# Cosformer attention and a mixture of adapters: K cast once, V weighted instead of K and Q, Q cast by GpSimd transfers, in a new schedule

## The chip, the cores and the metric

The kernel runs on one core of one Trainium2 chip. The metric is the time of one execution on the device, in microseconds (us); lower is better. The engines are named as in the profile: PE multiplies matrices (PEld is its weight load), DVE is the vector engine, ACT the scalar engine, POOL is GpSimd, and SP issues transfers. The transfers themselves are carried out by 16 DMA engines.

## The reference

The inputs q, k and v have the shape (8, 8, 576, 64): batches, heads, positions, features, in 32-bit floats. The attention is linear, and positions are weighted by a cosine and a sine. Its result is reshaped to 4608 rows of 512 features and goes through a mixture of eight low-rank adapters, of which each row takes its best two:

```python
theta = np.pi / 2.0 * pos / S
def phi(x, c, s):
    r = np.maximum(x, 0.0)
    return np.concatenate([r * c, r * s], axis=-1)
q_p, k_p = phi(q, cos_w, sin_w), phi(k, cos_w, sin_w)
kv  = np.einsum('bhsf,bhsd->bhfd', k_p, v)
num = np.einsum('bhsf,bhfd->bhsd', q_p, kv)
den = np.einsum('bhsf,bhf->bhs', q_p, k_p.sum(2))[..., None] + 1e-06
x = num / den                      # then to (4608, 512)
logits = x @ w_gate                # two largest of eight, softmax over the two: w
out = x + sum over the two e of w * ((x @ A[e]) @ B[e])
```

The sum over k_p is had by a column of ones beside v, so that kv has 65 columns.

## The kernel before

Position s is split as s = 9 p + j: p runs over 64 partitions (two heads fill 128), and j = 0 to 8 over the free dimension. A load (line 435, on SP's queue) brings q, k or v of one or two batches in this layout; one batch of one tensor is 1152 KB. The work goes by units of batches: [0], [1], [2,3], [4,5], [6,7] (line 20). For each unit the loads are K, V, Q in this order.

For each j of K and of Q a step `phi` multiplies by the cosine and by the sine of the position and writes bf16, two instructions of 256 columns (one batch) or 512 (two). For K it applies the relu as well, for Q not. It runs on ACT (line 487), DVE (490) or POOL (493). V is cast once, two instructions of 1152 columns a batch (`vc`, lines 360 to 362 by the engine), into `vb` with its column of ones. `kv` (line 540) is 72 matmuls a batch: 64 partitions of one head and one j contract 128 weighted features of K with 65 columns of V; both row halves of the array are used. `ke` copies kv out of PSUM.

The output is made in 36 tiles of 128 rows. A tile holds two blocks of 64 positions, from two batches or from two values of j. Per tile there are: `tq`, eight 128x128 transposes of weighted Q (line 650); `eq`, the relu on the way from PSUM to `qt`, 1024 columns a tile, mostly two tiles at a time (line 668, on DVE); `nd`, 16 matmuls of 65 columns in column halves of the array (line 691) and four narrow ones that add the epsilon (698); `rd` and `nx`, the reciprocal and the product into `x` (717, 722, DVE); `tx`, four transposes (742); `ex`, the copy into `xt` (358 on ACT, 362 on DVE); `za`, four matmuls with adapters A and gate (767). Then, for a group of up to three tiles, come the small steps of the choice of two: `mx` on DVE (778), `nt` on POOL (790), `ge` and `d` on DVE (799, 794), `sg`, a sigmoid, on ACT (804), `w` on POOL (807), `zg` on DVE (810). `tz` and `ez` transpose and copy the result; `dx` adds x and the adapters' output with two matmuls of 512 columns a tile (850, 852); `eo` copies the sum into `o` (358), and SP stores it (868). Matmuls at line 878 are fillers that keep PE busy in gaps.

The order is made by a planner (`plan`, line 124) that runs once, while the program is built: each step has engines with costs, buffers that it takes and frees, and a key; the planner simulates the engines and places what can start first. The result is one fixed order for each engine, and each engine works in that order, also when a step has to wait. A load is planned only when no more than 11.34 us of transfers are queued (`BACKLOG`, line 88). Staging for K and Q has two tiles of two batches each.

Of the kernel before, what the change touches and what calls it, by code (L numbers as in the profile page):

```python
# [14 lines left out]
AXL = mybir.AxisListType  # L15

NJ = 9
UNITS = [[0], [1], [2, 3], [4, 5], [6, 7]]  # L20
# [11 lines left out]
class Res:  # L32
    def __init__(self, name, n):
        self.name = name
        self.free = [0.0] * n
        self.held = [False] * n

    def reset(self):
        self.log = []
        self.free = [0.0] * len(self.free)  # L40
        self.held = [False] * len(self.held)

    def best(self, cnt, align, allowed=None):
        pick = None
        for s in range(0, len(self.free) - cnt + 1, align):
            if allowed is not None and s not in allowed:
                continue
# [24 lines left out]
class Op:  # L72
    def __init__(self, name, key, engs, deps, emit, alloc=(), free=(), dma=0):
        self.name, self.pos, self.engs, self.deps = name, key, engs, list(deps)
        self.emit, self.alloc, self.free, self.dma = emit, alloc, free, dma
        self.eng = None
        self.chain = None
        self.mode = 0
        self.sb = False
        self.pen = {}  # L80
        self.t0 = self.t1 = None
# [7 lines left out]
FILL_FROM = 4.0  # L89


EQ_TAIL, ND_TAIL, EX_TAIL, EO_TAIL = 2, 2, 2, 1
LAST_GROUPS = (3, 3, 2, 1)

A_TQ = {1: (4, 5, 6, 7), 2: (4, 6)}
A_ND = {1: (0, 2), 2: (0,)}
A_KV = (2, 4)
A_TX = (4, 5, 6, 7)
A_ZA = (6, 7)
A_TZ = (4, 5, 6, 7)  # L100
A_DX = (0, 1, 2, 3, 4, 5, 6, 7)
SWITCH = 0.1


KEYS = dict(
    phiK=17.14, phiKs=102.06, vc=72.58, kv=-11.86, ke=-59.38, phiQ=-13.35, phiQs=65.76,
    tq=-10.40, eq=30.86, nd=-2.33, rd=19.61, nx=-78.05, tx=-4.05, ex=-18.12, za=-6.99,
    mx=23.58, pqtA=76.06, pkP=0.00, pkD=-0.38, pqD=-0.74, pqA=0.45, pvD=-0.16, pvA=0.63,
    pxD=4.76, pzD=56.04, poD=0.76, rt=-122.12, sg=-18.44, zg=8.66, tz=-11.23, ez=-87.38,
    dx=-26.16, eo=-61.10, st=46.27,  # L110
)


TWEAK = {}


def place(o):
    if not isinstance(o.pos, tuple):
        return o.pos
    base, cls, x, slope = o.pos  # L120
    return base + KEYS[cls] + (x * KEYS[slope] if slope else x)


def plan(ops):
    for o in ops:
# [813 lines left out]
```

## Time and profile before

| | |
|---|---|
| median of three runs | 128.88 us (128.47, 129.69, 128.88) |
| span of the profiled execution, first to last instruction | 127.0 us |
| mean granted clock of PE | 0.987 |
| transferred | 38.60 MB; 28.85 MB read, 9.44 MB written in HBM |
| instructions | 4823 |

The profiled execution's own time isn't given apart from its span; the median stands 1.9 us above that span.

How the views are read. The page's slices cut the span into 40 equal parts; a digit is the busy share in tenths. A row of a group of instructions shows the line, the engine, the operation, output<-input with their shapes, the count, then "busy us, mean ns of one | idle time of the engine just before them <- what ended it". A row of windows shows the stretch, its length, each engine's busy time with the count of instructions, PE's clock, the share of time that the DMA engines were busy, and GB/s. A row of a timeline shows start, duration, engine, line and operation, and in brackets the idle time before it. The chain of work names, step by step back from the end, what the next step waited for. A row of the DMA queues shows packets, MB and the time the packets took, as a share of 16 engines' span.

### The profile page before, as it was taken

How to read it: one execution, taken by the hardware profiler on the slowest of the kernel's cores; microseconds unless marked ns; L12 is line 12 of the kernel's file. 1: busy time of each engine (PE TensorE's matmuls, PEld its weight loads, DVE VectorE, ACT ScalarE, POOL GpSimd, SP SyncE). 2: the span in 40 equal slices, each digit the busy share in tenths (PEclk: the TensorE clock that was granted, in tenths of full speed). 3: DMA queues.
4: the chain of work that ended last, by engine and by line, in shares of the span. 5: the costliest groups of instructions: out<-in, count | busy, mean ns of one | idle time of the engine just before them, and what ended most of it. 6: DMA issues, size and time to landing. Idle time of an engine off the chain costs nothing.

```text
span 127.0 us, 4823 instructions
## 1 busy us (share of the span) xinstructions
PE 104.9 (83%) x2068; PEld 75.4 (59%) x2068; DVE 99.1 (78%) x217; ACT 87.0 (68%) x151; POOL 52.2 (41%) x100
## 2 busy tenths in 40 slices
PE   2997889959878695698989794997899898899980
PEld 0335475637555574376877483685769768866520
DVE  0096999399989698959989997799898679976510
ACT  5072596895995565877997756697986543497950
POOL 5092803292481597107238990282592100111110
PEclk9999999999999999869999999999999999999999
DMA  3999999999999999999999999992233206004595
GB/s 73 410 395 390 392 329 384 391 391 396 387 391 390 393 403 396 414 392 393 407 398 408 399 393 390 407 392 84 124 132 155 98 5 246 7 0 177 223 376 222
DMA packets 16149, 38.60 MB, mean 304 GB/s; under 512 B 1792, under 2 KB 1792, under 8 KB 16128
## 3 DMA queue, kind: packets, MB, share of 16 engines
q1 hardware_dynamic: 16128, 38.29, 79.7%
q8 instruction: 16, 0.26, 0.8%
q14 instruction: 5, 0.04, 0.1%
HBM read 28.85 MB, written 9.44 MB: 301 GB/s over the span
## 4 chain that ended last, share of the span: by engine, by line
PE 36%; DVE 28%; DMA 23%; issue 5%; ACT 4%; SPq 2%; ACTq 0%; DVEq 0%
DMA q<-in_q_dram 23%; DVE qt L668 8%; DVE x L722 7%; DVE qp L490 7%; PE psum L650 7%; PE psum L850 6%; PE psum L852 5%; PE psum L540 4%; PE psum L742 4%; PE psum L767 4%; PE psum L691 3%; PE psum L878 2%; SPq L435 2%; ACT xt L358 2%; DVE rd L717 1%
## 5 line engine op out<-in xcount | busy, mean ns | idle before, releaser
L878 PE MATMUL psum<-ones,ident 128*128 128x512 bf16 x88 | 23.3, 398 | 3.0 <-POOL ident masks.py:199 2.5
L650 PE MATMUL psum<-ident,qp 128*128 128x128 bf16 x288 | 21.2, 222 | 3.4 <-DVE qp L490 1.5
L358 ACT COPY xt<-psum 128x1024 bf16<-128x1024 bf16 (+1 forms) x19 | 18.3, 964 | 8.1 <-PE psum L742 6.1
L487 ACT ACTIVATE kp<-k,cosw 128x512 bf16<-128x512 f32 (+1 forms) x31 | 19.2, 631 | 6.7 <-DMA k<-in_k_dram 6.7
L668 DVE TENSOR_SCALAR qt<-psum 128x2048 bf16<-128x2048 bf16 (+1 forms) x19 | 22.0, 1162 | 1.3 <-PE psum L650 1.0
L722 DVE TENSOR_TENSOR x<-psum,rd 128x1024 bf16<-128x1024 f32 (+1 forms) x19 | 22.2, 1168 | 0.6
L358 ACT COPY o<-psum 128x1024 f32<-128x1024 f32 (+1 forms) x22 | 18.0, 841 | 6.7 <-PE psum L852 6.5
L650 PEld LDWEIGHTS <-qp 128*128 128x128 bf16 x288 | 18.0, 99 | 5.6 <-issue 3.4
L493 POOL TENSOR_SCALAR qp<-q,cosw 128x512 bf16<-128x512 f32 (+1 forms) x22 | 15.5, 706 | 11.2 <-DMA q<-in_q_dram 11.2
L790 POOL TENSOR_TENSOR ss<-m 128x3 f32<-128x3 f32 (+2 forms) x15 | 2.9, 194 | 41.5 <-DVE m L778 41.3
L487 ACT ACTIVATE kp<-k,sinw 128x512 bf16<-128x512 f32 (+1 forms) x29 | 18.3, 640 | 0.0
L691 PE MATMUL psum<-kv,qt 128*64 128x65 bf16 x576 | 14.5, 196 | 3.7 <-issue 2.6
L691 PEld LDWEIGHTS <-qt 128*64 128x64 bf16 x576 | 12.5, 111 | 5.6 <-issue 3.0
L742 PE MATMUL psum<-ident,x 128*128 128x128 bf16 x144 | 12.0, 220 | 4.4 <-DVE x L722 3.4
L493 POOL TENSOR_SCALAR qp<-q,sinw 128x512 bf16<-128x512 f32 (+1 forms) x23 | 15.1, 663 | 0.0
L878 PEld LDWEIGHTS <-ident 128*128 128x128 bf16 x88 | 8.2, 102 | 11.6 <-issue 2.7
L850 PE MATMUL psum<-x,ident 128*128 128x512 bf16 x36 | 14.2, 393 | 1.2 <-ACT xt L358 0.8
L852 PE MATMUL psum<-Bb,zt 128*128 128x512 bf16 x36 | 14.1, 393 | 0.0
L360 POOL CAST vb<-v 128x1152 bf16<-128x1152 f32 x9 | 10.7, 1205 | 6.8 <-DMA v<-in_v_dram 6.8
L767 PE MATMUL psum<-AW,xt 128*128 128x136 bf16 x144 | 12.4, 228 | 1.1 <-ACT xt L358 0.8
L742 PEld LDWEIGHTS <-x 128*128 128x128 bf16 x144 | 9.4, 114 | 5.9 <-DVE x L722 4.5
L540 PEld LDWEIGHTS <-kp 64*128 64x128 bf16 x576 | 9.9, 94 | 4.2 <-issue 3.5
(45 smaller groups left out, 143.6 us busy)
## 6 DMA issues: line engine op xcount, KB each, us to landing
v<-in_v_dram SPq DMA_DIRECT2D x8, 1152.0 KB, 13.7
k<-in_k_dram SPq DMA_DIRECT2D x3, 2304.0 KB, 15.9
q<-in_q_dram SPq DMA_DIRECT2D x3, 2304.0 KB, 18.5
out_dram<-o SPq DMA_DIRECT2D x8, 768.0 KB, 4.2
out_dram<-o SPq DMA_DIRECT2D x10, 256.0 KB, 11.5
k<-in_k_dram SPq DMA_DIRECT2D x2, 1152.0 KB, 9.1
q<-in_q_dram SPq DMA_DIRECT2D x2, 1152.0 KB, 9.2
out_dram<-o SPq DMA_DIRECT2D x1, 512.0 KB, 2.6
```

The lines of the kernel that those rows point to most:

```text
L358: nc.scalar.copy(o_ap, i_ap)
L487: nc.scalar.activation(o_ap, i_ap, AF.Relu if isk else AF.Copy, bias=0.0, scale=tb)
L493: nc.gpsimd.tensor_scalar(out=o_ap, in0=i_ap, scalar1=tb, scalar2=0.0, op0=ALU.mult, op1=ALU.max if isk else ALU.add)
L650: nc.tensor.transpose(out=o_ap[:, hi, h2, :], in_=qv[:, bi * H2 + h2, :], identity=ident)
L668: nc.vector.tensor_scalar(out=o_ap, in0=i_ap, scalar1=0.0, scalar2=None, op0=ALU.max)
L691: nc.tensor.matmul(out=psum[hi * 64:hi * 64 + 64, s + g, x * W:(x + 1) * W], lhsT=qt[:, qi, hi, h2, hp * 64:hp * 64 + 64], rhs=kv_t[KV[b][ ...
L722: nc.vector.tensor_tensor(out=x_t[Y["x"].slot][:, 0:n].rearrange("p n (g i d) -> p (n g) i d", g=2, i=4), in0=f()[:, :, :, 0:D], in1=r().t ...
L742: nc.tensor.transpose(out=bank16(s, 1024)[:, i * 512 + c * 128:i * 512 + (c + 1) * 128], in_=xv[:, c, :], identity=ident)
L767: nc.tensor.matmul(out=psum[:, s, i * ZW:(i + 1) * ZW], lhsT=xt_t[Z["xt"].slot][:, zi, c, :], rhs=AW[:, c, :], start=(c == 0 and i == 0), ...
L850: nc.tensor.matmul(out=psum[:, s, :], lhsT=ident, rhs=x_t[Y["x"].slot][:, yi, :], start=True, stop=False)
L852: nc.tensor.matmul(out=psum[:, s, :], lhsT=zt_t[Gd["zt"].slot][:, i, :], rhs=Bb, start=False, stop=True)
L878: nc.tensor.matmul(out=psum[:, s, :], lhsT=ident, rhs=warm, start=True, stop=True, skip_group_check=True)
```

## The change

The weights move from K and Q to V. K is cast with its relu once per batch, in two instructions of 1152 columns (`kr`). V is written twice, times cosine and times sine, with cosine and sine in the place of the ones (`vw`, `vbc`). A kv matmul then contracts 64 features of K with 130 columns, in quarters of the array (`kv`). Q is loaded as bf16 by transfers that POOL issues and that cast on the way (`LQ`), for two batches at a time. It is transposed without weights (`tq`, 64 columns of weights to an instruction); the copy from PSUM applies the relu (`eq`, 1024 columns for two tiles). The sine part is made from it in SBUF by a multiply with the tangent (`tn`, on DVE or POOL), so that rows carry Q and Q times tangent; numerator and denominator lack the cosine, which drops out of the quotient, and the epsilon is divided by the cosine to match (`epsT`). The numerator's matmuls use row halves of the array.

All batches now go in pairs: five groups per pair, four of two tiles and one of one tile. A tile of the larger groups holds one batch and two values of j; `dx` puts the rows back in order with twice as many matmuls, each of 64 output rows in a column half. The loads are K0, V0, K1, V1, Q01, and then K, V, Q for each further pair. K and V share eight staging slots, each of one batch, Q has two tiles of a pair. `o` has six buffers of two tiles for three of three. The weights come in nine transfers for three. The planner has new keys and, for most steps, a correction of its own (`PEN`, `TWEAK`).

```diff
-UNITS = [[0], [1], [2, 3], [4, 5], [6, 7]]
+LOADS = [
+    ("K", [0]), ("V", [0]), ("K", [1]), ("V", [1]), ("Q", [0, 1]),
+    ("K", [2, 3]), ("V", [2, 3]), ("Q", [2, 3]),
+    ("K", [4, 5]), ("V", [4, 5]), ("Q", [4, 5]),
+    ("K", [6, 7]), ("V", [6, 7]), ("Q", [6, 7]),
+]
+NST, NKB, NQS, NQT, NX, NXT, NZT, NO, NKV, NRD, NSM = 8, 8, 2, 3, 4, 2, 2, 6, 4, 2, 3
...
+            if nm == "Q":
+                K.nc.gpsimd.dma_start(out=K.qs[G[nm, P]["s"].slot], in_=src)
+                return
+            s = G[nm, bs[0]]["s"].slot if nm == "K" else G[nm, P]["s"].slot + bs[0] % 2
+            K.nc.sync.dma_start(
+                out=K.st[s // 2][:, (s % 2) * H2:(s % 2 + nb) * H2, :], in_=src)
...
+    def relu(e, o_ap, i_ap):
+        nc = K.nc
+        if e == "ACT":
+            nc.scalar.activation(o_ap, i_ap, AF.Relu)
+        elif e == "POOL":
+            nc.gpsimd.tensor_scalar(out=o_ap, in0=i_ap, scalar1=BIG, scalar2=0.0,
+                                    op0=ALU.min, op1=ALU.max)
+        else:
+            nc.vector.tensor_scalar(out=o_ap, in0=i_ap, scalar1=0.0, scalar2=None, op0=ALU.max)
...
+    def e_rc(e):
+        K.nc.vector.reciprocal(K.rcT, K.cosT)
+
+    def e_tan(e):
+        nc = K.nc
+        nc.vector.tensor_tensor(out=K.tanT, in0=K.sinT, in1=K.rcT, op=ALU.mult)
+        nc.vector.tensor_scalar(out=K.epsT, in0=K.rcT, scalar1=1e-6 / 64.0, scalar2=None,
+                                op0=ALU.mult)
...
+    def e_vbc(e):
+        for s in range(NJ + VB_SECOND):
+            K.nc.gpsimd.tensor_copy(
+                K.vb[s][:, :, :, D],
+                K.cs[:, s % NJ, :].unsqueeze(1).broadcast_to([128, 2 * H2, 2]))
...
+                    relu(e, K.kb[T["k"].slot],
+                         K.st[h // 2][:, (h % 2) * H2 + 2 * c:(h % 2) * H2 + 2 * c + 2, :])
...
+                        if e == "ACT":
+                            nc.scalar.activation(o_ap, i_ap, AF.Copy, bias=0.0, scale=tb)
+                        else:
+                            (nc.vector if e == "DVE" else nc.gpsimd).tensor_scalar(
+                                out=o_ap, in0=i_ap, scalar1=tb, scalar2=0.0,
+                                op0=ALU.mult, op1=ALU.add)
...
+                                K.nc.tensor.matmul(
+                                    out=K.psum[x * 64:x * 64 + 64, s + hp, i * 2 * W:(i + 1) * 2 * W],
+                                    lhsT=kt[hp * 64:hp * 64 + 64, x, j * D:(j + 1) * D],
+                                    rhs=K.vb[VB[j]["v"].slot][hp * 64:hp * 64 + 64,
+                                                              bi * H2 + h2, :, 0:W],
...
+                                K.nc.tensor.transpose(
+                                    out=ov[xs, i, :, bi, :] if one else ov[xs, bi, i, :, jj, :],
+                                    in_=qs[:, 4 * bi + 2 * i + x, j * D:(j + 1) * D],
+                                    identity=K.ident)
...
+                relu(e, K.qt[Q["qt"].slot][:, 0, 0:cols_of(nj)], K.bank16(Q["ps"].slot, cols_of(nj)))
...
+                (K.nc.vector if e == "DVE" else K.nc.gpsimd).tensor_tensor(
+                    out=qt[:, 1, 0:cols_of(nj)].rearrange("p (g c) -> p g c", c=c),
+                    in0=qt[:, 0, 0:cols_of(nj)].rearrange("p (g c) -> p g c", c=c),
+                    in1=K.tanT[:, j0 * 64:j0 * 64 + c].unsqueeze(1).broadcast_to([128, 8, c]),
+                    op=ALU.mult)
...
+                                for f in range(2):
+                                    for x in range(2):
+                                        xs = slice(x * 64, x * 64 + 64)
+                                        nc.tensor.matmul(
+                                            out=K.psum[o0:o0 + on, s + x,
+                                                       (2 * i + hp) * W:(2 * i + hp + 1) * W],
+                                            lhsT=(qv[xs, f, i, hp, half, :] if one
+                                                  else qv[xs, f, half, i, hp, :]),
+                                            rhs=kv[xs, hp, i, f, :],
...
+                for jj in range(2):
+                    for bi in range(2):
+                        nc.tensor.matmul(out=K.psum[bi * 64:bi * 64 + 64, s + jj, :],
+                                         lhsT=K.ident[:, jj * 64:jj * 64 + 64],
+                                         rhs=xs[:, bi, :].rearrange("p (x i c) -> p i x c", x=2, i=2),
+                                         start=True, stop=False, skip_group_check=True)
+                    for bi in range(2):
+                        nc.tensor.matmul(out=K.psum[bi * 64:bi * 64 + 64, s + jj, :],
+                                         lhsT=zt[:, bi * 128 + jj * 64:bi * 128 + jj * 64 + 64],
+                                         rhs=K.Bb, start=False, stop=True, skip_group_check=True)
```

More of the change, by code (lines that the diff above doesn't have):

```diff
@@ L165, in plan @@
             ready(o)
+    order = []
     while avail:
@@ L377, in e_ident @@
-    def e_ident(e):
-        make_identity(nc, ident)
-    def e_misc(e):
-        nc.gpsimd.memset(ones, 1.0)
-        nc.gpsimd.memset(epsr, 1e-6 / 128.0)
-        for t in vb_t:
-            nc.gpsimd.memset(t[:, :, :, D:W], 1.0)
-    o_half = add("half", -100, {"DVE": 0.1}, [], e_half)
-    o_pos = add("pos", -100, {"POOL": 0.6}, [], e_pos)
-    o_tab = add("tab", -100, {"ACT": 2.0}, [o_half, o_pos], e_tab)
-    o_misc = add("misc", -99, {"POOL": 1.2}, [], e_misc)
-    o_ident = add("ident", -98, {"POOL": 1.5}, [], e_ident)
@@ L872 @@
-    order = plan(ops)
-    def e_fill(e, n, s):
-        for _ in range(n):
-            nc.tensor.matmul(out=psum[:, s, :], lhsT=ident, rhs=warm,
-                             start=True, stop=True, skip_group_check=True)
+    def relu(e, o_ap, i_ap):
[7 more added lines that the diff above has]
+            nc.vector.tensor_scalar(out=o_ap, in0=i_ap, scalar1=0.0, scalar2=None, op0=ALU.max)
@@ new lines, in e_ident @@
+    def e_ident(e):
+        make_identity(K.nc, K.ident)
+        K.nc.gpsimd.memset(K.ones, 1.0)
+    def e_vbc(e):
[3 more added lines that the diff above has]
+                K.cs[:, s % NJ, :].unsqueeze(1).broadcast_to([128, 2 * H2, 2]))
+    o_half = add("half", "", -100, {"DVE": 0.1}, [], e_half)
+    o_pos = add("pos", "", -100, {"POOL": 0.9}, [], e_pos)
+    o_tab = add("tab", "", -100, {"ACT": 2.0}, [o_half, o_pos], e_tab)
```

1039 lines of the change are left out of this document (470 added, 569 removed), and 119 rows, old and new, of tables (KEYS, PEN, TWEAK).

## The prediction

> **What bounds the kernel now.** First the page: busy time, two rows of its slices, its chain.
>
> ```profile
> PE 104.9 (83%) x2068; PEld 75.4 (59%) x2068; DVE 99.1 (78%) x217; ACT 87.0 (68%) x151; POOL 52.2 (41%) x100
> ...
> DVE  0096999399989698959989997799898679976510
> GB/s 73 410 395 390 392 329 384 391 391 396 387 391 390 393 403 396 414 392 393 407 398 408 399 393 390 407 392 84 124 132 155 98 5 246 7 0 177 223 376 222
> ...
> PE 36%; DVE 28%; DMA 23%; issue 5%; ACT 4%; SPq 2%; ACTq 0%; DVEq 0%
> ```
>
> Until slice 27 (about 86 us) the transfers run at some 395 GB/s; then they nearly stop, and the kernel still computes for 41 us. The windows put numbers on both halves (columns: PE, PEld, DVE, ACT, POOL busy, clock, DMA share, GB/s); the timelines of POOL and SP show why the border is there.
>
> ```profile
> 24.00:86.00 62.00, 50.74 (x1146) 38.77 (x1145) 55.25 (x115) 47.21 (x77) 33.90 (x55) 0.97 1.04 396
> 86.00:127.00 41.00, 34.38 (x679) 25.46 (x671) 28.64 (x68) 26.31 (x44) 8.92 (x23) 1.00 0.35 142
> ```
> ```profile
> 85.10 1.36 POOL L493 TENSOR_SCALAR qp<-q,cosw 128x512 bf16<-128x512 f32 x2 [0.63 <-DMA q<-in_q_dram]
> ```
> ```profile
> 65.13 3.56 SPq L435 DMA_DIRECT2D q<-in_q_dram  x1
> 72.35 52.15 SPq L868 DMA_DIRECT2D out_dram<-o  x10
> ```
>
> The last load, Q of batches 6 and 7, is issued at 65.1 and lands at about 85. Before it two limits meet: the transfers are full, and DVE is busy 55.3 of 62 us. So computing is behind when the loads end, and the 41 us after them are a backlog (PE 34.4 busy): the lines of that window hold 21 of the 36 residual matmuls, one per tile.
>
> ```profile
> L850 PE MATMUL psum<-x,ident 128*128 128x512 bf16 x21 | 7.9, 378 | 0.4 <-DVE qt L668 0.3
> ```
>
> So some 18 to 21 tiles are unfinished when the last load lands. A gain must come from a smaller backlog at 85, and from a cheaper tail.
>
> **The element work.** The tile views of k, q, v and qt, in this order, give what the casts, weightings and the relu cost (k and v: DVE, ACT or POOL; the first two numbers in the qt row are PE's).
>
> ```profile
> 0.00:127.00 127.00, 13.31 (x27) 34.65 (x60) 3.54 (x3) 0.99 0.81 304
> ...
> 0.00:127.00 127.00, 18.87 (x37) 4.39 (x8) 30.14 (x45) 0.99 0.81 304
> ...
> 0.00:127.00 127.00, 5.90 (x7) 10.72 (x9) 0.99 0.81 304
> ...
> 0.00:127.00 127.00, 14.52 (x576) 12.48 (x576) 22.00 (x19) 0.99 0.81 304
> ```
>
> Removed: K twice 51.5, Q twice 53.4, V once 16.6, the copy of qt 22.0: together 143.5 us. Added: K once, 16 instructions of 1152 columns, by the v row 16.6; V twice, as many columns as K twice, 52.5 (the mean of k and q); the qt copy at half its columns 11.0. That leaves 63.4 less, before the tangent. Groups are now of two tiles (20 for 15), so five more sets of small steps, some 1 us each: +5.
>
> ```profile
> L722 DVE TENSOR_TENSOR x<-psum,rd 128x1024 bf16<-128x1024 f32 x17 | 20.8, 1224 | 0.6
> L358 ACT COPY xt<-psum 128x1024 bf16<-128x1024 bf16 x17 | 17.2, 1010 | 8.1 <-PE psum L742 6.1 <-DVE m L778 1.6
> L358 ACT COPY o<-psum 128x1024 f32<-128x1024 f32 x13 | 13.1, 1011 | 6.0 <-PE psum L852 5.9
> L493 POOL TENSOR_SCALAR qp<-q,cosw 128x512 bf16<-128x512 f32 x16 | 12.3, 770 | 5.0 <-DMA q<-in_q_dram 5.0
> L778 DVE MAX8 m<-psum 128x8 f32<-128x8 f32 x36 | 5.0, 164 | 3.8 <-PE psum L767 3.5
> L717 DVE RECIPROCAL rd<-psum 128x16 f32<-128x16 f32 x17 | 4.3, 251 | 2.7 <-PE psum L698 2.4 <-ACT ex L804 0.3
> L493 POOL TENSOR_SCALAR kp<-k,cosw 128x256 bf16<-128x256 f32 x3 | 3.5, 1191 | 3.9 <-DMA k<-in_k_dram 3.9
> L493 POOL TENSOR_SCALAR qp<-q,cosw 128x256 bf16<-128x256 f32 x6 | 3.2, 538 | 6.2 <-DMA q<-in_q_dram 6.2
> L810 DVE TENSOR_TENSOR zg<-psum,w 128x256 bf16<-128x256 f32 x5 | 2.1, 420 | 1.0 <-POOL w L807 0.8
> L807 POOL TENSOR_TENSOR w<-ge,ex 128x24 f32<-128x24 f32 x8 | 2.0, 255 | 3.4 <-ACT ex L804 3.4
> L358 ACT COPY zt<-psum 128x256 bf16<-128x256 bf16 x5 | 1.8, 369 | 2.3 <-PE psum L826 2.3
> L668 DVE TENSOR_SCALAR qt<-psum 128x1024 bf16<-128x1024 bf16 x2 | 1.4, 680 | 0.0
> L799 DVE TENSOR_TENSOR ge<-psum,m 128x16 f32<-128x16 f32 x5 | 0.9, 175 | 0.2
> L794 DVE SCALAR_TENSOR_TENSOR d<-psum,ss 128x16 f32<-128x16 f32 x5 | 0.8, 169 | 0.3 <-POOL ss L790 0.2
> L807 POOL TENSOR_TENSOR w<-ge,ex 128x8 f32<-128x8 f32 x2 | 0.4, 203 | 1.0 <-ACT ex L804 1.0
> ```
>
> Tangent multiply: 16 of 1024 columns and 4 of 512, SBUF to SBUF, on DVE or POOL; no row shows it. On DVE it lies between the 680 ns of a qt copy and the 1224 ns of x. On POOL between 1.5 us (two tensor_scalar of 512 at 770) and 3.5 us: w rises by 52 ns over 16 elements, 3.25 ns each, times 1024, plus its base. I take 1 us, nearest to the wide one-pass rows: 18 in all; both ends stay for the range. The multiply is also a new link: PE's numerator matmuls now wait for it as well as for the relu, and what stands behind them in PE's order waits too, about 1 us later per group. Three qt buffers let the relu and the multiply run a group ahead, which covers it except in the last group, where I count it. Net: 238.3 us of DVE, ACT and POOL now, less 63.4, plus 18 and 5: 198.
>
> Set-up: a reciprocal and two multiplies over 576 columns, two sines, 14 small POOL copies into vb, together some 10 us. DVE's first wait covers DVE's share (5.4 us until K lands at 6.2); POOL's copies must be over before V's first weighting, where V now lands at about 9.5. I cost them at nothing; without that cover V's first weighting, and kv of batch 0 behind it, come some 2 us later, early on, where the transfers set the pace. The first output starts later, since Q comes behind K and V of two batches; loads go on meanwhile, so nothing.
>
> PE, from the chain in order of time:
>
> ```profile
> 95.26 0.24 PE psum L767 x4
> 95.50 2.43 PE psum L540 x144
> ...
> 98.27 0.45 PE psum L650 x8
> 98.71 0.22 PE psum L742 x4
> 100.02 0.28 PE psum L691 x16
> 101.69 0.38 PE psum L850
> 102.06 0.22 PE psum L852
> ```
>
> A tile costs 0.45 (transposes), 0.28 to 0.37 and a little (numerator), 0.22, 0.24, 0.43 (the pair of wide ones): 1.7 to 1.9, two tiles 3.4 to 3.8. In the new layout transposes, kv and numerator use quarters or halves of the array: unchanged at worst, half the transposes at best, so 3.0 to 3.8 per group. The wide residual and adapter matmuls become twice as many, in column halves; the 16 narrow ones in 0.28 us (17 ns each, where 128 columns take 56) show that halves overlap, so equal; if not, +0.86 a group.
>
> **The transfers.**
>
> ```profile
> q1 hardware_dynamic: 16128, 38.29, 79.7%
> ```
>
> 79.7% of 16 engines over 127 us are 1620 us for 16128 packets: 100 ns each. Q is 4096 of them, now issued by POOL (four, for five on SP) and written as bf16. SP keeps ten loads of K and V; the weights come in nine issues for three, stores in 20 for 19, at SP's cost, which waits mostly anyway. A cast packet: 50 ns if the written half counts, 150 if reading and writing no longer overlap, perhaps more. I take 100, since as much is read. Then the loads end when they do now, 85: the bytes are the same, and as much of the output is stored meanwhile as now, about 4 MB of 9.4 (390 GB/s over 83 us are 32.4 MB, loads 28.9). Buffers don't hold the loads: K's staging is free after one cast, and Q's third transfer needs only pair zero's transposes, of Q that lands at about 22, while its turn on the transfers comes only after two pairs are loaded, at about 40 (14.2 MB at 395 GB/s). Two queues also share the engines, so a Q load may overtake V's and V land late; V's weighting, kv and its copy then stand in front of the numerator. I cost this at nothing while the backlog of loads is two pairs deep; if it bites in the last pair, half a transfer, 3 us. On POOL's queue a Q load stands behind what waits there:
>
> ```profile
> POOL ss L790 <- DVE m L778: 41.3, 13, 8.7
> ```
>
> A wait of up to 8.7 us can hold it back; the transfers have about 11 us of work queued by the planner, which covers this.
>
> POOL and DVE hinder each other: the same 128x256 form takes POOL 538 ns, and 1191 in the start where DVE works on k. A page speaks against the change here. The Trainium skill, "SBUF — State Buffer", section "The 'DVE blocks DMA' trap (SWDGE)", says that GpSimd can't write descriptors while DVE holds the shared port, and that a DMA of 620 ns then takes 3100. By that rule the last Q comes 2.5 us later and the sum below would be 116.7; no run here shows it yet.
>
> **The sum.** Tail after 85: pair three's nine tiles, five groups. A group costs DVE 1.22+0.25+0.33+0.18+0.17+0.42+0.68 = 3.25, ACT 1.01+0.37+1.01 and the sigmoid, 2.6, PE 3.0 to 3.8: pace 3.4. The fifth group starts at 85+13.6 = 98.6; transposes, relu, tangent and numerator of its one tile take 2.5. The rest is measured at the end of the kernel now:
>
> ```profile
> 115.81 0.20 DVE L717 RECIPROCAL rd<-psum 128x8 f32<-128x8 f32 x1
> ```
> ```profile
> 123.56 0.58 ACT L358 COPY o<-psum 128x512 f32<-128x512 f32 x1 [0.58 <-PE psum L852]
> ```
>
> From that reciprocal to the end of o: 8.3; to the span's end 2.9 more. 98.6+2.5+8.3+2.9 = 112.3 of span. Around this span lie 1.9 us to the median 128.9 (the runs, 128.5 to 129.7, would make it 1.5 to 2.7), so **114.2**. A second way agrees: until 86 the three engines did 174 of their 238 us; of 198 and 10 for set-up 34 are left, and at the tail's pace now (63.9 in 41, 1.56 per us) they take 22, with 2.9 for the last store a span of 111.
>
> **Rivals.**
> - Cheap casts: 50 ns a packet saves 4096 x 50 / 16 = 12.8 us of transfers. Loads end at 72; but at 2.2 us of work per us (136.4 in 62) only 143 of 208 are then done, and 65 at up to 2.2 take 29: with the store 104 of span, **106**. For: half the bytes land. Against: the reads are unchanged.
> - POOL becomes late: the multiply costs 3.5 us there. POOL then needs 4 us a group in the tail (+2.4 over four), the last group 1.2 longer, and the Q issues wait in its queue, about 2: **120**. For: the w rows. Against: DVE can take it. The Trainium skill, "GPSIMD Engine Reference", section 3.1, has a two-input floor of 2.6 cycles per element, by estimate 2.2 us at 1024 and 1.2 GHz; the sum would be 117 by it, and the w rows lie above it.
> - Slower: a cast packet costs twice, 200 ns. Loads end 25.6 us later, 137.9 of span, **140**. It decides from 14.7 us up, that is at 157 ns a packet. For: no row shows a cast. Against: the plain packets' 100 ns, and that reading sets it.
> - No change: the loads' end again finds 18 tiles unfinished, because POOL, DVE and ACT wait for each other in their fixed order, and PE takes them at 1.9 each: 85+34+8 = 127 of span, **129**. Against: DVE's 89% before 86 would fall to some 75%.
>
> **Chances.** The forecast's case 0.52 (109 to 119), cheap casts 0.15, POOL late 0.15, slow casts 0.15, no change 0.03. The time is that of the likeliest; 104 to 127 leaves out the slow casts and a little at both ends. A measurement of this kernel tells 1% from no change. Faster 0.82, within 1% 0.03, slower 0.15.
>
> **What would show it.** Right: no phi of q in the trace; DVE well under 89% between 24 and 86; last load at about 85; pace of x near 3.4 after it. Wrong: packets on a new queue over 100 ns; POOL multiplies over 2 us; transfers with gaps before 80; V's weighting waiting on V while engines stand; PE over 3.8 a group.

## The result, and the profile after

The changed kernel takes 137.53 us (median of four runs, 136.15 to 138.88), the kernel before, timed beside it, 128.68: a ratio of 1.0625, 95% interval 1.0536 to 1.0714. It is slower by 6%; 114.2 was forecast. Executions fall into two groups, the slower one at a lower clock, and every ratio here compares the faster groups alone: for the changed kernel these are the runs of 136.15 and 136.58. The profiled execution took 136.15 us, with a span of 134.4.

From the page of the changed kernel: busy time, transfer rate in its 40 slices, the two queues, the chain.

```profile
PE 106.2 (79%) x2149; PEld 68.3 (51%) x2149; DVE 78.7 (59%) x188; ACT 71.5 (53%) x120; POOL 94.5 (70%) x143
...
GB/s 87 409 365 290 290 283 119 297 398 283 290 294 342 407 391 392 405 318 281 279 367 409 391 372 291 164 191 235 12 137 24 312 5 66 176 5 79 222 242 164
...
q1 hardware_dynamic: 12656, 28.85, 58.2%
q0 software_dynamic: 4160, 4.72, 20.9%
...
DMA 30%; POOL 28%; PE 17%; issue 7%; ACT 6%; DVE 6%; SPq 2%; POOLq 0%; ACTq 0%; DVEq 0%
```

DVE and ACT lost 36 us of busy time, POOL gained 42: the three together have 244.7, where 208 were forecast and 238.3 stood before. After PE, at 79%, POOL is the busiest with 70%. The timeline of x, one row per group (first and last of each pair of batches), shows how the output comes:

```profile
35.32 1.23 DVE L744 TENSOR_TENSOR x<-psum,rd 128x1024 bf16<-128x1024 f32 x1
48.96 0.69 DVE L744 TENSOR_TENSOR x<-psum,rd 128x512 bf16<-128x512 f32 x1
61.52 1.23 DVE L744 TENSOR_TENSOR x<-psum,rd 128x1024 bf16<-128x1024 f32 x1
75.86 0.69 DVE L744 TENSOR_TENSOR x<-psum,rd 128x512 bf16<-128x512 f32 x1
85.90 1.22 DVE L744 TENSOR_TENSOR x<-psum,rd 128x1024 bf16<-128x1024 f32 x1
100.31 0.69 DVE L744 TENSOR_TENSOR x<-psum,rd 128x512 bf16<-128x512 f32 x1
110.53 1.21 DVE L744 TENSOR_TENSOR x<-psum,rd 128x1024 bf16<-128x1024 f32 x1
123.22 0.69 DVE L744 TENSOR_TENSOR x<-psum,rd 128x512 bf16<-128x512 f32 x1
```

Inside a pair five groups come in 13 to 14 us, 3.2 to 3.6 a group. Between the last x of a pair and the first of the next lie 12.6, 10.0 and 10.2 us. At 85 us not five groups are left, as forecast, but ten. From the reciprocal ahead of the last x (at 122.97) to the end of the span it is 11.4 us, where 11.2 was forecast (8.3 and 2.9). So the whole miss, 22 us of span, lies ahead of the last x.

Groups by shape, and the issues of SP and POOL, show three terms that came out otherwise than costed:

```profile
L684 POOL TENSOR_TENSOR qt<-qt,tanT 128x1024 bf16<-128x1024 bf16 x15 | 32.8, 2196 | 12.8 <-ACT qt L428 12.8
L595 POOL TENSOR_SCALAR vb<-st,cs 128x512 bf16<-128x512 f32 x32 | 22.1, 699 | 1.2 <-DMA st<-in_v_dram 1.2
L593 ACT ACTIVATE vb<-st,cs 128x512 bf16<-128x512 f32 x14 | 9.6, 714 | 1.5 <-DMA st<-in_v_dram 1.5
L595 DVE TENSOR_SCALAR vb<-st,cs 128x512 bf16<-128x512 f32 x8 | 7.2, 900 | 0.0
L684 POOL TENSOR_TENSOR qt<-qt,tanT 128x512 bf16<-128x512 bf16 x4 | 4.8, 1197 | 0.0
L684 DVE TENSOR_TENSOR qt<-qt,tanT 128x1024 bf16<-128x1024 bf16 x1 | 1.8, 1802 | 0.4 <-ACT qt L428 0.4
```
```profile
21.36 0.32 SPq L493 DMA_DIRECT2D o<-in_moe_w_gate_dram  x1
22.74 0.35 SPq L495 DMA_DIRECT2D o<-in_moe_B_dram  x1
23.14 0.43 SPq L529 DMA_DIRECT2D st<-in_k_dram  x1
```
```profile
80.65 0.96 POOL L526 DMA_DIRECT2D qs<-in_q_dram  x1
```

The multiply went to POOL 19 times of 20 and takes 2.2 us there. The nine weight issues hold SP until 22.7 us, so K of batches 2 and 3 is issued at 23.1, and the rate drops to 119 GB/s in the slice from 20 us. Q's last load is issued at 80.65. Each of the three looks like a cause. The experiments asked which of them is one.

### The profile page after: what moved, and what is told of

It is laid out like the page before. It is cut to its first block, busy times and chain, and to the rows that moved or that the text cites. A ratio compares the mean times of both kernels' runs of the same rounds, so it can differ in the third digit from the quotient of the medians.

```text
span 134.4 us, 4959 instructions
## 1 busy us (share of the span) xinstructions
PE 106.2 (79%) x2149; PEld 68.3 (51%) x2149; DVE 78.7 (59%) x188; ACT 71.5 (53%) x120; POOL 94.5 (70%) x143
## 3 DMA queue, kind: packets, MB, share of 16 engines
q1 hardware_dynamic: 12656, 28.85, 58.2%
q0 software_dynamic: 4160, 4.72, 20.9%
## 4 chain that ended last, share of the span: by engine, by line
DMA 30%; POOL 28%; PE 17%; issue 7%; ACT 6%; DVE 6%; SPq 2%; POOLq 0%; ACTq 0%; DVEq 0%
DMA st<-in_v_dram 16%; POOL qt L684 15%; DMA o<-in_moe_A_dram 15%; POOL vb L595 10%; PE psum L711 3%; ACT qt L428 3%; PE psum L855 3%; ACT o L419 3%; PE psum L860 2%; PE psum L830 2%; DVE zg L815 2%; SPq L529 2%; PE psum L755 2%; DVE x L744 2%; POOL ss L795 2%
## 5 line engine op out<-in xcount | busy, mean ns | idle before, releaser
L684 POOL TENSOR_TENSOR qt<-qt,tanT 128x1024 bf16<-128x1024 bf16 (+1 forms) x19 | 37.5, 1986 | 12.8 <-ACT qt L428 12.8
L595 POOL TENSOR_SCALAR vb<-st,cs 128x512 bf16<-128x512 f32 (+1 forms) x45 | 28.7, 649 | 5.6 <-DMA st<-in_v_dram 5.6
L593 ACT ACTIVATE vb<-st,cs 128x256 bf16<-128x256 f32 (+1 forms) x29 | 15.8, 601 | 15.9 <-DMA st<-in_v_dram 15.9
L428 ACT ACTIVATE qt<-psum 128x1024 bf16<-128x1024 bf16 (+1 forms) x15 | 14.5, 971 | 11.9 <-PE psum L669 7.8
L711 PE MATMUL psum<-kv,qt 64*128 64x65 bf16 (+1 forms) x640 | 15.4, 194 | 4.1 <-POOL qt L684 2.2
L621 PE MATMUL psum<-vb,kb 64*64 64x130 bf16 x576 | 12.4, 230 | 6.4 <-POOL vb L595 4.2
L595 DVE TENSOR_SCALAR vb<-st,cs 128x256 bf16<-128x256 f32 (+1 forms) x16 | 10.7, 700 | 9.9 <-DMA st<-in_v_dram 9.9
L430 POOL TENSOR_SCALAR kb<-st 128x1152 bf16<-128x1152 f32 x11 | 13.5, 1234 | 4.0 <-DMA st<-in_k_dram 4.0
L711 PEld LDWEIGHTS <-qt 64*128 64x128 bf16 (+1 forms) x640 | 12.5, 98 | 6.8 <-POOL qt L684 2.5
L855 PE MATMUL psum<-x,ident 128*64 128x512 bf16 x64 | 13.0, 402 | 0.1
L860 PE MATMUL psum<-Bb,zt 128*64 128x512 bf16 x64 | 12.7, 393 | 0.0
L419 ACT COPY zt<-psum 128x256 bf16<-128x256 bf16 (+1 forms) x17 | 6.0, 352 | 12.4 <-PE psum L830 11.4
## 6 DMA issues: line engine op xcount, KB each, us to landing
st<-in_k_dram SPq DMA_DIRECT2D x3, 2304.0 KB, 13.5
st<-in_v_dram SPq DMA_DIRECT2D x2, 1152.0 KB, 13.5
```

Source lines behind the costliest of these rows:

```text
L419: nc.scalar.copy(o_ap, i_ap)
L428: nc.scalar.activation(o_ap, i_ap, AF.Relu)
L593: nc.scalar.activation(o_ap, i_ap, AF.Copy, bias=0.0, scale=tb)
L595: (nc.vector if e == "DVE" else nc.gpsimd).tensor_scalar(out=o_ap, in0=i_ap, scalar1=tb, scalar2=0.0, op0=ALU.mult, op1=ALU.add)
L621: K.nc.tensor.matmul(out=K.psum[x * 64:x * 64 + 64, s + hp, i * 2 * W:(i + 1) * 2 * W], lhsT=kt[hp * 64:hp * 64 + 64, x, j * D:(j + 1) * D ...
L684: (K.nc.vector if e == "DVE" else K.nc.gpsimd).tensor_tensor(out=qt[:, 1, 0:cols_of(nj)].rearrange("p (g c) -> p g c", c=c), in0=qt[:, 0, ...
```

## The experiments

Each run's ratio is that to the kernel before, timed beside it on the same chip; 1.0625 is the changed kernel's. The expectations name theories by letters: P, the multiply on POOL; Q, the hole in the transfers behind the weight issues; T, and later L, a chain of steps that wait for each other; S, two queues that share the transfers; O, the fixed order of each engine; E, the wait for whole pairs of loads.

**The multiply on DVE**, at its old place in the order:

```diff
-            o.emit(o.eng)
+            o.emit("DVE" if o.cls == "tn" else o.eng)
```

> All twenty tangent multiplies are issued on DVE, at the same place in the order; nothing else changes. Theory P (the multiply's 2.2 us on POOL, and what queues behind it there, make the kernel late): POOL falls from 94.5 to about 57 us busy, DVE rises from 78.7 to about 110 if each multiply costs 1.8 us there as the single one of the changed kernel did; the time falls by 8 to 12 us, from 137.5 to 126-130. Theory Q (the early hole in the transfers, because nine weight issues hold SP's queue until 22.7 us, makes everything late): 0 to 2 us less. Theory T (the end is a chain of nine unfinished groups that wait for each other, whichever engine multiplies): 1 to 3 us less, or even more time, since DVE then becomes the engine that others wait for.

Measured: 134.67 us, 1.0507 (1.0407 to 1.0608). POOL falls to 58.6 us of busy time, and 1% is gained, not the 6 to 9% that P expected. The chain of waits of this run has another head:

```profile
PE 35%; DVE 24%; DMA 15%; POOL 10%; issue 8%; ACT 4%; SPq 1%; DVEq 0%; POOLq 0%
```

POOL's 28% were real waits, but the next engine stood right behind. Theory P falls as the main cause.

**One input in place of two**, on the same engine (times 0.5, plus 0; the sine part is left out):

> The tangent multiply is replaced on the same engine and at the same place by an instruction that reads one tensor in place of two (times 0.5 and plus 0), so the sine part of the weighting is left out and the output is not the reference's. Theory P, with two inputs as the cause of the 2.2 us: the instruction takes 1.1 to 1.4 us at 1024 columns (POOL's 512-column weightings take 0.65), POOL falls by 15 to 20 us of busy time, and the time falls by 6 to 10 us, to 127-131. If it takes 2.2 us with one input too, the number of inputs is not the reason. Theory Q: 0 to 2 us less. Theory T: 1 to 3 less.

Measured: 131.96, 134.01, 134.09 and 134.16 us, where the kernel before took 128.77. These runs are too scattered for a ratio; 2 to 4 us are gained, less than the 6 to 10 that P expected.

```profile
L683 POOL TENSOR_SCALAR qt<-qt 128x1024 bf16<-128x1024 bf16 x15 | 16.0, 1066 | 15.9 <-ACT qt L428 15.8
```

1066 ns for 2196: without the second input it takes half. The instruction is another one too (`tensor_scalar` for `tensor_tensor`, with no broadcast operand), so the run doesn't show that the number of inputs alone doubles it.

**The weight loads behind V of batches 2 and 3**, alone and with the multiply on DVE:

```diff
+    at = {o.name: o for o in order}
+    order.remove(at["ldw"])
+    order.insert(order.index(at["LV2"]) + 1, at["ldw"])
```

> The nine weight issues are moved on SP's queue behind the loads of K and V of batches 2 and 3; nothing else changes. Theory Q: the load of K of batches 2 and 3 is issued before 10 us in place of 23.1, the slice with 119 GB/s at 20 to 23.5 us fills up, the last load lands 3 to 7 us earlier and the time falls by 3 to 7 us, to 131-135. Theory P: the loads come earlier, but POOL takes the work no faster: 0 to 2 us less. Theory T: the same, 0 to 2.

> The edits of the multiply on DVE and of the later weight issues together. P and Q both true and independent: the sum of the two runs' gains, 11 to 17 us, 120-126. If only P is true, as the run with the multiply on DVE alone; if only Q is true, as the run with the later weights alone. If T is true, less than 4 us: 133.5 or more.

Measured: 147.56 us, 1.1512 (1.1407 to 1.1618), and 146.22, 1.1417 (1.1307 to 1.1526). The edit moved a load and not the step that waits for it. From the waits of the first of the two:

```profile
DVE AW L499 <- DMA o<-in_moe_B_dram: 18.0, 1, 18.0
```

DVE's cast of the weights stands early in its fixed order; it waited 18 us, and all of DVE behind it. This says nothing on Q, but a lot on fixed orders.

**SP with four weight issues**: the gate weights (two issues) and B go on POOL's queue ahead of Q's first load.

> The four loads of adapter weights A stay on SP's queue; the gate weights (two issues in place of four) and B are issued by POOL just ahead of Q's first load, so SP has four weight issues in place of nine and nothing else is moved. Theory Q as the trace suggests it (SP's ninth and later transfers wait until the one eight before them has landed, so nine weight issues hold K of batches 2 and 3 until V of batch 1 is in): that load is issued at 5 to 10 us in place of 23.1, the hole at 20 to 24 us (0.59 DMA share) closes, V of batches 2 and 3 lands 2 to 3 us earlier, and the time falls by 2 to 4 us, to 133.5-135.5. Theory O (the engines' fixed order, made for a cheaper multiply and for transfers that come one after the other, is what holds the kernel, so that a transfer that comes a little earlier finds the engines not ready): 0 to 1.5 us less.

Measured: 136.28 us, 1.0550 (1.0465 to 1.0634). Windows from 20 to 24 us, the changed kernel and this run (DMA share and GB/s are the last two numbers), and SP's issue here:

```profile
20.00:24.00 4.00, 1.01 (x18) 0.58 (x17) 2.06 (x5) 2.63 (x7) 2.56 (x6) 0.85 0.59 121
```
```profile
20.00:24.00 4.00, 0.71 (x16) 0.48 (x16) 1.93 (x4) 2.30 (x6) 2.24 (x5) 0.92 1.18 246
```
```profile
14.00 0.45 SPq L532 DMA_DIRECT2D st<-in_k_dram  x1
```

The hole is closed, K's load goes out 9 us earlier, and nothing that can be measured is gained. Theory Q falls.

**Q's first load later**, behind POOL's last cast of K of batch 1:

> Q's first load is issued by POOL behind its last cast of K of batch 1, at some 13 us in place of 4.4; nothing else changes. Theory S (two queues share the transfer engines, and Q's load has pushed V of batch 1 back): V of batch 1 lands at 15 to 16 us in place of 20.7, K of batches 2 and 3 is issued at 16 to 18 in place of 23.1, Q lands at 26 to 28 in place of 18. If the late V was what made the kernel late, the first x comes at 31 to 33 us in place of 35.3 and the time falls by 3 to 8 us. Theory O, or if the transfers as a whole set the pace: the first x comes at 34 to 36 and the time changes by less than 1.5 us. If no sharing takes place, V of batch 1 lands where it did.

Measured: 135.51 us, 1.0407 (1.0288 to 1.0526). V of batch 1 is issued at 2.31; its landing (last column) in the changed kernel and in this run:

```profile
st<-in_v_dram SPq DMA_DIRECT2D x1, 1152.0 KB, 19.0
```
```profile
st<-in_v_dram SPq DMA_DIRECT2D x1, 1152.0 KB, 13.5
```
```profile
30.85 1.22 DVE L744 TENSOR_TENSOR x<-psum,rd 128x1024 bf16<-128x1024 f32 x1
```

The two queues do share: V lands 5.5 us earlier, and the first x comes at 30.85 for 35.32. At the end 2% are left of it, between what S (3 us or more) and O (under 1.5) expected.

**Loads left out.** In the changed kernel those of batches 4 to 7 (`if P >= 2: return` in the load step); then all but batches 0 and 1, from which all pairs are computed; and in the kernel before those of batches 6 and 7:

> The loads of K, V and Q of batches 4 to 7 are left out (14.2 MB, some 37 us of transfers); the engines work in the same order on the data of batches 0 to 3 that is still in the buffers, so the outputs of batches 4 to 7 are not the reference's. If the transfers set the pace of the changed kernel after the first two pairs, as they did before 86 us in the kernel before and as its transfers busy until 95 us suggest, the last x comes 15 us earlier or more and the time falls to 115-122. Theory O (each engine's fixed order, with a multiply that takes twice its planned time in it, sets the pace from the landing of V of batches 2 and 3 on): the time stays within 2 us of 136.5, because nothing that the late loads release is next in any engine's order.

> The changed kernel with the loads of batches 0 and 1 alone (7.1 MB); all four pairs are computed from their data, in the same order, so the outputs of batches 2 to 7 are not the reference's. No transfer is waited for after some 21 us. If the landing of the second pair (V of batches 2 and 3 at 44.7) is what makes the changed kernel late, as the chain of waits through it suggests, the time falls by 8 us or more, to 128 or less. Theory O (fixed order and engines): the four pairs take their 24 us each whatever lands, and the time stays within 2.5 us of 136.5.

> The kernel before the change, without the loads of batches 6 and 7 (7.1 MB, 18 us of transfers); the engines work in the same order on data of earlier batches, so the outputs of batches 6 and 7 are not the reference's. If the full transfers bounded the kernel until 86 us, as the prediction has it, the work of the last two batches is free to start 10 us or more earlier and the time falls by 6 to 12 us, to 117-123. If the engines' fixed order is the bound and the loads run ahead of it, the time stays within 1.5 us of 128.8. The transfers that are full until 86 us would then bound neither kernel.

Measured: 135.77 us, 1.0488 (1.0409 to 1.0567); 135.33, 1.0449 (1.0302 to 1.0596); the kernel before without its last loads 127.36, 0.9920 (0.9873 to 0.9966). The rates of the first and the third:

```profile
GB/s 84 411 368 292 290 281 120 284 403 299 295 290 265 18 39 117 237 158 172 0 0 5 0 156 165 158 149 90 5 9 148 199 123 111 131 5 114 199 236 159
```
```profile
GB/s 61 407 398 390 396 339 368 396 387 391 392 390 392 392 395 404 410 395 392 404 277 5 5 252 5 126 131 0 248 12 248 9 62 195 5 0 234 211 388 182
```

After 43 us, or after 65, the transfers idle most of the time, and both kernels end nearly where they did. Full transfers were no bound of either, by themselves.

**Work left out.** V's weighting of batches 2 to 7; then also the multiplies to DVE; then also kv and its copy (`if P >= 1: return` in these steps, which then use batches 0 and 1). In the kernel before, the sine halves of K and Q of batches 4 to 7:

> V's weighting is left out for batches 2 to 7 (54 of 72 weightings, some 41 us of POOL, ACT and DVE); their kv is made from the weighted V of batches 0 and 1, so their outputs are not the reference's. The prediction's second way (busy time of the three engines, done at 1.56 us per us) gives 41/1.56, 26 us less, 110. Theory O, where POOL is the chain (23 of the 41 us lie on POOL): 12 to 20 us less, 117-124. Theory L (the steps of a group wait for each other through five engines, and the work left out filled waits of that chain): 2 to 8 us less, 129 or more.

> As the run without V's weighting for batches 2 to 7, and the multiplies on DVE: POOL falls to some 36 us of busy time, DVE stays near 80, ACT near 60. If POOL was what is left in that run, 5 to 10 us less than it. Theory L: within 3 us of it, and no engine but PE is busy for 70% of the span.

> As that, and the kv products and their copies of batches 2 to 7 are left out too (8 us of PE's 77 without fillers, 6 copies); the numerators of all pairs use kv of batches 0 and 1. So no pair waits for its V or K. If the chain V, weighting, kv, numerator makes the gaps of 10 to 12 us between the last x of a pair and the first of the next, these gaps close to 4 us or less and the time falls by 15 us or more under the run before it. Theory L: the gaps stay at 7 us or more, since the engines' fixed order puts the other steps there, and 2 to 6 us are gained.

> The kernel before the change, with the sine halves of K and Q of batches 4 to 7 left out (36 instructions, some 25 us of DVE, ACT and POOL after 45 us); the old sine halves in the buffers are used, so the outputs of batches 4 to 7 are not the reference's. By the prediction's second way (1.56 to 2.2 us of work done per us) the time falls by 11 to 16 us, to 113-118. Theory L (the chain of steps through the engines in their fixed order sets the pace, in the kernel before too): 0 to 5 us less, 124 or more.

Measured: 133.43 us, 1.0367 (1.0079 to 1.0656); 133.25, 1.0364 (1.0153 to 1.0575); 128.18, 0.9899 (0.9650 to 1.0149); the kernel before with less work 128.53, 1.0003 (0.9957 to 1.0049). Busy time of the third and the fourth:

```profile
PE 98.8 (79%) x1717; PEld 61.4 (49%) x1717; DVE 79.5 (64%) x193; ACT 63.0 (50%) x106; POOL 37.2 (30%) x92
```
```profile
PE 106.8 (84%) x2068; PEld 76.0 (59%) x2068; DVE 92.2 (72%) x207; ACT 78.2 (61%) x136; POOL 43.7 (34%) x89
```

The interval of the third is wide. In it 65 us of the three engines' 244.7 are gone, and 7% of the time; in the kernel before 24 us of 238.3 are gone (99.1, 87.0 and 52.2 were 92.2, 78.2 and 43.7), and nothing. The busy time of these three engines, by itself, was no bound either. What L expected came in all four; in the third run the gaps between pairs are still 8 to 13 us.

**No fillers on PE:**

> The 105 filler matmuls (28.9 us of PE's busy time) are left out; nothing else changes. If fillers that stand in PE's fixed order at places where the chip is late hold the real matmuls back, the time falls by 3 to 8 us. If they keep the granted clock up and fit into waits, the mean clock falls under 0.90 and the time rises by 2 us or more. Theory O (POOL and the chain of one pair set the pace): within 2 us either way.

Measured: 139.11 us, 1.0845 (1.0698 to 1.0993), the mean clock 0.921 where the changed kernel's was 0.953. The fillers do not hold the work back; without them it is some 2% slower, though the two intervals still touch. PE is busy 87.3 of 137.0 us in this run, so PE alone does not fill the changed kernel's time.

**A new order.** The planner gets the durations of the trace, and its keys are searched anew; in the second also the split weights, in the third also V loaded ahead of K:

```diff
-                     {"DVE": d_sb(cols), "POOL": p_cp(cols)}, [eq, o_tan]
+                     {"DVE": 0.15 + cols / 1920.0, "POOL": 0.10 + cols / 500.0}, [eq, o_tan]
```

> The same steps, loads, buffers and nine weight issues, but a new order: the planner gets the durations that the trace of the changed kernel shows (multiply of 1024 columns 2.15 us on POOL and 0.68 on DVE, K's cast 1.16 on POOL), and its keys and corrections are searched anew for them; 14 of the 20 multiplies go to DVE. Theory O: the order was the matter, and the time falls by 7 to 11 us, to 126-130, about the kernel before. Theory E (whole pairs of loads must land before anything can be computed from them, so engines starve for the first 40 us and are late at the end whatever the order): at most 4 us, 133 or more.

> As the replanned order, with the gate weights and B issued by POOL as in the run with the weights split. The order was searched for this form. Theory O: 2 to 3 us under the replanned one with nine issues on SP, 124-128, because now an order made for early loads finds them early. Theory E: as that run, within 1 us.

> As the replanned order with the split weights, but V is loaded ahead of K for batches 2 to 7, since V has 18 weightings a pair and K four casts; the order is searched anew for it. If V's weighting behind its landing is the chain that makes each pair late, V of batches 6 and 7 lands 8 us earlier, its weighting is over by 85 to 90 in place of 103, and the time falls to 122-127. If not, as the replanned order, 126-130.

Measured: 136.56 us, 1.0454 (1.0337 to 1.0571); 135.15, 1.0458 (1.0387 to 1.0529); 133.04, 1.0296 (1.0229 to 1.0364). Each gains less than O expected. In the first two it is E's expectation that came, at most 4 us under the changed kernel and no difference between them. V first is the best version that computes the reference, and does not reach the kernel before.

**The same with one pair's data**, the planner told that nothing more is loaded:

> The changed kernel with the loads of batches 0 and 1 alone, as in the run with one pair's data, but with an order made for it: the planner is told that nothing more is loaded, gets the durations of the trace, and its keys are searched anew (15 of 20 multiplies on DVE). The outputs of batches 2 to 7 are not the reference's. Theory O (the order is the matter, made for other landings): 118-123, and the gaps between pairs shrink to 6 us. Theory L (five groups a pair, one after the other through five engines, whatever the order): 125 or more, with the pace inside a pair at 3 us and more.

Measured: 118.29 us, 0.9222 (0.9152 to 0.9293), with a mean clock of 0.994. Its busy time, and the x of its pairs, first and last:

```profile
PE 97.6 (84%) x2134; PEld 65.6 (56%) x2134; DVE 81.4 (70%) x195; ACT 76.2 (66%) x128; POOL 69.1 (59%) x125
```
```profile
30.30 1.23 DVE L1286 TENSOR_TENSOR x<-psum,rd 128x1024 bf16<-128x1024 f32 x1
44.28 0.68 DVE L1286 TENSOR_TENSOR x<-psum,rd 128x512 bf16<-128x512 f32 x1
54.35 1.22 DVE L1286 TENSOR_TENSOR x<-psum,rd 128x1024 bf16<-128x1024 f32 x1
69.14 0.68 DVE L1286 TENSOR_TENSOR x<-psum,rd 128x512 bf16<-128x512 f32 x1
73.97 1.23 DVE L1286 TENSOR_TENSOR x<-psum,rd 128x1024 bf16<-128x1024 f32 x1
87.17 0.69 DVE L1286 TENSOR_TENSOR x<-psum,rd 128x512 bf16<-128x512 f32 x1
93.47 1.22 DVE L1286 TENSOR_TENSOR x<-psum,rd 128x1024 bf16<-128x1024 f32 x1
104.07 0.69 DVE L1286 TENSOR_TENSOR x<-psum,rd 128x512 bf16<-128x512 f32 x1 [0.52 <-PE psum L1397]
```

The same steps on the same data in the old order took 135.33 (1.0449). The gaps between pairs are now 10.1, 4.8 and 6.3 us. The time is what O expected: by the ratios the new order is worth 16 us here. Order means more than sequence in this: some steps have other engines (15 of 20 multiplies on DVE, worth some 1.5 us by the first run, and all of K's casts on POOL), and the clock is 0.994 for 0.961. O and L are one theory then, as far as these runs tell: the steps wait for each other in the order that they are given.

Neither half does it alone. One pair's data in the old order is 2% faster than the changed kernel, a new order with all loads 2 to 3%, the two together 13%.

## Why the prediction was wrong

- **What bounds the kernel: wrong, and this step carries the miss.** The prediction read full transfers and a DVE busy 89% as two limits, and took what is removed from them off the time. Without the last 7.1 MB the kernel before gains 0.8%; without 24 us of element work, nothing. Its chain, in order of time, could have warned: its last wait for a transfer ends at 42.5 us, half way through the full transfers.

```profile
24.05 18.47 DMA q<-in_q_dram
```

  What the runs of the changed kernel show in the place of these limits: each engine works through a fixed list, whose steps wait for each other across five engines, and busy time that is taken out of it leaves a wait in its place (65 us out, 9 us gained). The Trainium skill, "Perfetto Trace Analysis", section "Identifying the Most-Contended Engine", says to optimize the engine of the highest occupancy first, and for PE to go by weight loads and the share of peak in place of busy time. Here DVE was the busiest element engine at 78%, above PE's weight loads (59%), and 6.9 us less of it, with 17 us less of ACT and POOL, moved nothing.
- **PE was left out of the limits.** For the kernel before, the fixed list has a rival that no run took away. From 86 to 120 us, PE is busy 30.87 of 34 us, and the fillers (second row) are 0.73 of it:

```profile
86.00:120.00 34.00, 30.87 (x664) 24.22 (x657) 27.47 (x64) 23.76 (x39) 8.52 (x21) 1.00 0.27 107
```
```profile
86.00:120.00 34.00, 0.73 (x3) 0.31 (x4) 1.00 0.27 107
```

  With the sine halves left out PE has 30.87 us in this window again. So element work may have gone for nothing there because PE was nearly full. In the changed kernel PE's matmuls without fillers fill 27.2 of these 34 us. They also start later: by 45 us PE has done 17.9 us of them in the kernel before, 10.9 in the changed kernel, 16.8 in the run of 118 us.
- **The sum of element work: its sign did not matter, its size was off.** V twice was costed at 52.5 and took 55.2 (28.7, 15.8 and 10.7 on POOL, ACT and DVE); the multiply was costed at 18 and took 39.3, since the planner, which prices it at 1.15 on POOL, sent 19 there. The copy of qt took 17.3 for 11.0 and K's cast 19.6 for 16.6. The upper bound, 3.5 on POOL, was too high, and 2.2, the estimate by the Trainium skill's "GPSIMD Engine Reference", section 3.1, was right: the trace agrees with 2196 ns. For the kernel's time, the rival of a late POOL gave 5.8 us, the sum by the page 2.8; the run with the multiply on DVE gives 1.5 by the ratios.
- **The tail: the pace right, the count wrong.** This is the term of the sum that was mis-sized. 3.4 a group was forecast, 3.2 to 3.6 came. The count, five groups, took for granted that pairs zero to two are done when the last load lands. The forecast had 13.6 and 2.5 us from 85 on; the trace has 14.4 for pair two from 85.9 on, a gap of 10.2, and 12.7 for pair three. That is the 22 us. In the gap V of the last pair is weighted, made into kv and copied, in an order where the last groups of the pair before stand between. V's landing (2304 KB, issued at 61.54) and POOL's first and last weightings of it:

```profile
st<-in_v_dram SPq DMA_DIRECT2D x1, 2304.0 KB, 18.8
```
```profile
90.64 1.52 POOL L595 TENSOR_SCALAR vb<-st,cs 128x512 bf16<-128x512 f32 x2
...
100.79 2.19 POOL L595 TENSOR_SCALAR vb<-st,cs 128x512 bf16<-128x512 f32 x3
```

  It lands at 80.3, and its weighting ends at 103. But this work only fills the gap: with the weighting, kv and its copy left out, 8.4 us of it stayed.
- **Costed at nothing, and seen:** the nine weight issues make the hole, Q overtakes V by 5.5 us, Q's last load waits in POOL's queue. Its buffer was free at 62.4, with the last transposes of pair one, and it went out at 80.65: a wait of 18 us, where up to 8.7 was reckoned with. It landed 13.5 us later, at 94.2, where the sum had the loads end at 85. In the fixed order each is worth 0 to 2%, as the runs with four issues, with Q later and without late loads show. The price was near, though not for the reason given, that a backlog of loads hides them.
- **Cast packets: right.** 20.9% of 16 engines over 134.4 us for 4160 packets is 108 ns each, 99 for the others (58.2%, 12656). The rivals of cheap and of slow casts both fall; that the slow one's 140 lies nearest to the measured time is chance. The 2.5 us by the Trainium skill, "SBUF — State Buffer", aren't seen either: POOL's four issues took 0.96 to 1.10 us, and no run here shows them held up by DVE.
- **The rival of no change** had the mechanism, engines that wait for each other in their fixed order, and got 3 in 100, on the ground that DVE's 89% would fall. It fell to 63% (38.4 of 61 us from 24 to 85), and that proved nothing. Its number, 129, was too low as well.

What stays open: with all loads in place no order found here came under a median of 133 us, while without them one came to 118. The chain of V first waits for K of batches 2 and 3 until 43.2 us and for no transfer behind it:

```profile
9.47 33.74 DMA st<-in_k_dram
```

From there to its end it is 89 us; in the run of 118 us it is 90 from its chain's last landing, at 26.0. So between these two the difference lies ahead of that landing. But in the replanned order with nine issues the chain's last landing is at 19.1, and 117 us follow; which landings an order must be built around was not taken apart. Nor were loads and work left out of the old order together, in either kernel, so two limits that each hold when the other is gone are not excluded; and no run of the kernel before made PE's own work smaller.

## What to carry to other kernels

In a kernel whose engines each follow a fixed list, busy shares and full transfers do not tell what a removed instruction is worth; ask which steps then start earlier in the list, or leave the instruction out, make the list anew and compare the two lists on the same data. Look at every engine for the bound, the matrix engine without its fillers too. Count the backlog by the units that the new layout makes ready at once (here a pair of batches, with a chain ahead of its first output), not by the tiles of the old one. When a load is moved, move the step that waits for it too.

## What the runs showed of the hardware

The tangent multiply on DVE reads two tensors in SBUF. Beside an idle POOL it takes 0.67 us; beside POOL's casts of K and a weighting, recorded from 0.02 us later on, it took 3.49. From the timeline of the run with the multiply on DVE:

```profile
78.53 0.67 DVE L684 TENSOR_TENSOR qt<-qt,tanT 128x1024 bf16<-128x1024 bf16 x1
```
```profile
55.82 3.49 DVE L684 TENSOR_TENSOR qt<-qt,tanT 128x1024 bf16<-128x1024 bf16 x1
```
```profile
55.84 2.26 POOL L430 TENSOR_SCALAR kb<-st 128x1152 bf16<-128x1152 f32 x2
58.08 0.68 POOL L595 TENSOR_SCALAR vb<-st,cs 128x512 bf16<-128x512 f32 x1
```

The Trainium skill, "SBUF — State Buffer", section "Who interferes with whom", has it that a DVE instruction with two inputs in SBUF contends with a GpSimd instruction that reads SBUF, and that the second one is blocked until the first is done. The length agrees: the 3.49 us end at 59.31, 0.55 us after POOL's three instructions (58.76), which is about the time that the multiply takes alone. Who came first the trace doesn't settle: by the recorded starts it was DVE, by 0.02 us.

The small weight loads hold SP's queue here. SP's twelfth transfer, the last gate weight, was issued at 21.36, when V of batch 1, the fourth, had just landed (2.31 and 19.0 make 21.3). With four weight issues the load of K that had been fourteenth was ninth and went out at 14.00. What they wait for stays open: a limit of eight transfers under way would fit the first number, but in the second run the fifth to eighth issue already took from 3.13 to 13.96.
